# Batch 0's states alone ahead of x, identity products between TensorE's early steps, VectorE's order kept into batch 1, and stores of the state rows by quarters

## The chip, the cores and the metric

The kernel runs on one core of one Trainium2 chip. A core has five engines with a queue of instructions each: TensorE (PE in the profile; PEld is its loading of the stationary operand), VectorE (DVE), ScalarE (ACT), GpSimd (POOL) and SyncE (SP), which here only issues transfers. Engines run at the same time and wait for one another through semaphores; each works through its own queue in order. The metric is the device time of one execution in microseconds, as the median of several runs. The profile is of one execution.

## The reference

Two blocks are joined. The first reads x (8 batches, 8 heads, 512 tokens, 64 values) and 32 states per batch and head; the second is a feed-forward layer over 4608 rows.

```python
scores = scale * x @ state.T;  a = softmax(scores);   xread = a @ state     # 512 rows per batch
scores2 = scale * state @ x.T; a2 = softmax(scores2); sread = a2 @ x        # 32 rows per batch
x = concat([xread, sread], rows), heads side by side                        # (8*544, 512)
h = x @ w_in                                                                # 512 -> 2048
g = where(h > 0, h, exp(min(h, 0)) - 1)
out = g @ w_out                                                             # 2048 -> 512
```

The two weight matrices arrive as 64-bit numbers (a 128x512 piece is 512 KB); everything is computed in 32 bits.

## The kernel before, in words

A batch's 512 token rows go through attention, a first product (`ffn1`, 16 parts `F:0` to `F:15` of 128 hidden columns) and a second product with w_out. The states are folded into the first product: M = states x w_in (`make_m`), copied to `m_sb` (`copy_m`, `copy_half`), is multiplied by the turned attention weights `aT`. After each part ScalarE makes the exponential (`exp_part`, two ACTIVATEs), and VectorE the maximum (`max_part`, into `g_all`). Nearly every instruction is recorded at the helper's line L100, so rows are told apart by their tiles.

**Batch 0** (`first_batch`) runs while the weights arrive. Its order is written out by hand as a list, `plan`, and TensorE, VectorE, ScalarE and GpSimd keep that order (`InOrder`). The steps, for batch b and half g:

- `kT`, `kTc`: turn the states on TensorE, copy them to `kT` on VectorE. `x:b.i`, `xc:b.i`: turn half of x, copy on ScalarE. `sc`: scores. `mx`, `tr`, `tm`: column maximum, transpose, row maximum on VectorE; `ps`, `pm`: subtract and scale on GpSimd; `ae`, `te`: exponentials on ScalarE; `sd`, `su`: sums and reciprocals on VectorE; `tt`: transpose to `aT`. `sT`, `sTc`, `sr`, `src`: turn the state-side weights, copy, multiply by x, keep.
- `w:k.1`, `w:k.2`: conversion of weight piece k, three ScalarE and four VectorE instructions. After each `w:k.2` comes `fetch`, which issues one more piece on SP's queue. Pieces 0-3 are w_in for parts 0-3, 4-7 for parts 4-7, 8-11 the first four of w_out, and so on.
- `M`, `Mc`: M for two parts, and its copy. `F`, `R`, `E`, `O`: a part of the first product, its exponential, its maximum, and its share of the second product, which adds into banks 0 to 3 (`ffn2_row`).

At the end banks 0 to 3 are copied to `o_sb` and stored.

**Batches 1 to 7** (`batch`) do all 16 parts of the first product, then the second product by Strassen's scheme (`Strassen`, and in it `Second`), which needs sums and differences of quarters of w_out (`weight_sum` into `t_w`, and `Second.weights` into `t`, `b` and parts of w_in). Those are made in batch 1. `F` parts of batch 1 rotate through banks 4, 5, 3. In the second product, the attention of the next batch is put between its steps (`attention`, `hooks`). From batch 1 on VectorE, ScalarE and GpSimd no longer keep the written order: a scheduler may pull a ready instruction forward. TensorE and SP keep theirs throughout.

**The state rows** of all batches come last (`states`): one first product, one Strassen product of seven products in two halves of 256 rows (`half.o_sb[0]`, `[1]`), and eight stores on SP's queue, one a batch.

TensorE's pair of banks 6 and 7 is shared by the turned states, x, scores, the half M's and the state read of batch 0, so each of these steps waits for the copy of the one before.

Of the kernel before, what the change touches and what calls it, by code (L numbers as in the profile page):

```python
# [10 lines left out]
FP32 = mybir.dt.float32  # L11
# [14 lines left out]
def kernel(  # L26
# [15 lines left out]
    B, H, S, D = x.shape  # L42
    NS = state.shape[2]
    DM, DF = moe_w_in.shape
    P = 128
# [39 lines left out]
    def bank(i):  # L85
        return psum[:, i]

    def pair(i):

        return psum[:, i : i + 2]  # L90
# [19 lines left out]
    def transpose(out, in_):  # L110


        for t in range(2):
            rows = slice(t * 64, (t + 1) * 64)
            tensor.transpose(out[:, t], in_[rows], ident[rows, rows], tile_position=(t * 64, 0))
# [22 lines left out]
                out=x_t[b][:, r].rearrange("p (h d) -> p h d", d=D), in_=x_v[:, r]  # L138
            )

    def load_states():
        raw = work.tile([P, B, G, D], FP32, tag="w", name="s_sb")
        s_v = state.rearrange("b (m c) n d -> m c n b d", c=G)
        for m in range(NP):
            for c in range(G):
                (sync, scalar)[c].dma_start(out=raw[m * NS : (m + 1) * NS, :, c], in_=s_v[m, c])
        return raw

    def turn_states(raw):
        ps = st["k_ps"] = pair(6).rearrange("p t (b q) -> p t b q", q=64)  # L150
        for b in range(B):
            transpose(ps[:, :, b], raw[:, b].rearrange("p c d -> p (c d)"))

    def load_weights(src):
        _, n, k = src.shape
# [281 lines left out]
    def combine(out, x, y, op=ALU.subtract):  # L437
        for o, i, j in zip(out, x, y):
            vector.tensor_tensor(out=o, in0=i, in1=j, op=op)
# [3 lines left out]
    b11, b12, b21, b22 = (halves(w_k[:, :, e, h]) for e in range(2) for h in range(2))  # L443
    t_w = {3: b12}

    def weight_sum(i):

        if i != 3:
            t_w[i] = [
                work.tile([P, FO // 4, DM // 2], FP32, tag="w", name="t_w") for k in range(2)  # L450
            ]
        x, y = {1: (b12, b11), 2: (b22, t_w.get(1)), 3: (b22, b12), 4: (b21, t_w.get(2))}[i]
        combine(t_w[i], x, y)

    class Second:

# [232 lines left out]
    def first_batch():  # L689

        plan = """
            kT kTc x:0.0 xc:0.0 w:0.1 x:0.1 xc:0.1 w:0.2 w:1.1 sc:0 mx:0.1 w:2.1 tr:0.1 tr:0.0
            tm:0.1 w:3.1 tm:0.0 ps:0.1 mx:0.0 w:1.2 ps:0.0 ae:0.1 ae:0.0 te:0.1 sT:0 sd:0.0 sd:0.1
            te:0.0 su:0.1 sTc:0 su:0.0 pm:0.1 w:4.1 M:0.0.0 w:3.2 pm:0.0 Mc:0.0.0 w:7.1 sr:0 tt:0.1
            tt:0.0 w:4.2 F:0 src:0 w:8.1 w:2.2 F:1 R:0 w:5.1 E:0 M:0.0.1 w:8.2 Mc:0.0.1 R:1 F:2  # L700
            w:5.2 w:9.1 O:0 E:1 w:10.1 w:9.2 R:2 F:3 w:10.2 w:6.1 M:0.1.0 O:1 E:2 Mc:0.1.0 w:6.2 R:3
            w:12.1 E:3 F:4 w:7.2 w:11.1 O:2 w:12.2 w:13.1 R:4 w:11.2 M:0.1.1 F:5 w:14.1 w:13.2 O:3
            R:5 Mc:0.1.1 E:4 w:16.1 E:5 w:14.2 F:6 w:17.1 M:0.2.0 w:16.2 F:7 R:6 w:15.1 E:6 O:4
            w:17.2 Mc:0.2.0 w:18.1 w:15.2 F:8 R:7 w:18.2 O:5 w:21.1 E:7 R:8 w:21.2 M:0.2.1 w:19.1
            O:6 E:8 w:23.1 w:19.2 Mc:0.2.1 F:9 w:23.2 w:24.1 O:7 w:25.1 w:24.2 w:20.1 w:25.2 F:10
            R:9 O:8 w:20.2 w:22.1 E:9 R:10 w:22.2 M:0.3.0 w:26.1 F:11 E:10 O:9 Mc:0.3.0 w:26.2 R:11
            w:27.1 E:11 M:0.3.1 w:29.1 w:27.2 F:12 O:10 R:12 w:29.2 Mc:0.3.1 w:30.1 E:12 F:13 w:31.1
            w:30.2 O:11 R:13 w:31.2 w:28.1 E:13 x:1.0 w:28.2 F:14 xc:1.0 x:1.1 R:14 F:15 xc:1.1 E:14
            sc:1 R:15 O:12 mx:1.0 mx:1.1 ae:1.0 tr:1.0 ae:1.1 tr:1.1 tm:1.0 sT:1 tm:1.1 ps:1.0 O:13
            sd:1.0 sTc:1 sd:1.1 E:15 ps:1.1 te:1.0 su:1.0 te:1.1 pm:1.0 su:1.1 sr:1 pm:1.1 tt:1.0  # L710
            O:14 src:1 tt:1.1 M:1.0 O:15 Mc:1.0
        """.split()
        make_identity(nc, ident)
        o_ps = [bank(c) for c in range(R)]
        order = [lambda k=k: load_w_in(0, k) for k in range(4)]
        for c in range(1, FC + 1):
            if c < FC:
                order += [lambda c=c, k=k: load_w_in(c, k) for k in range(4)]
            order += [lambda fo=fo: load_w_out(fo) for fo in range(4 * c - 4, 4 * c)]
        w, h, e = [], {}, {}  # L720

        def fetch():
            if len(w) < len(order):
                w.append(order[len(w)]())
            elif 1 not in x_t:
                load_x(1, [sync])
                for c in range(FC):
                    k = slice(2 * c, 2 * c + 2)
                    sync.dma_start(out=w_in_mem[:, k], in_=w_in[:, k])

        raw_states = load_states()
        load_x(0, [sync, scalar])
        for k in range(NRAW - 1):
            fetch()
        groups = {
            "mx": column_max, "tr": turn_scores, "ae": column_exp, "tm": row_max,
            "ps": row_subtract, "te": row_exp, "su": row_sum, "pm": row_scale,
            "tt": turn_tokens, "sd": column_total,
        }
        whole = {  # L740
            "sc": scores, "sT": turn_state, "sTc": copy_state, "sr": state_read,
            "src": keep_read,
        }
        for step in plan:
            name, _, num = step.partition(":")
            num = [int(i) for i in num.split(".") if i]
            if name == "kT":
                turn_states(raw_states)
            elif name == "kTc":
                vector.tensor_copy(out=kT.rearrange("p b (t q) -> p t b q", t=2), in_=st["k_ps"])  # L750
                fetch()
            elif name in groups:
                groups[name](*num)
            elif name in whole:
                whole[name](*num)
            elif name == "w":
                (convert_1, convert_2)[num[1] - 1](*w[num[0]])
                if num[1] == 2:
                    fetch()
            elif name == "F":  # L760
                h[num[0]] = ffn1(0, num[0])
            elif name == "R":
                e[num[0]] = exp_part(h[num[0]])
            elif name == "E":
                max_part(num[0], e[num[0]], h[num[0]])
            elif name == "O":
                ffn2_row(o_ps, num[0])
            elif name == "x":
                turn_x(*num)
            elif name == "M":  # L770
                make_m(*num)
                if len(num) == 2:
                    make_m(1, 1, first=4)
            elif name == "xc":
                copy_x(*num)
            else:
                assert name == "Mc", step
                if len(num) == 3:
                    copy_half(*num)
                else:  # L780
                    for g in range(G):
                        copy_m(*num, g, scalar.copy)
        for g in range(G):
            copy_m(1, 1, g, scalar.copy)
        for i in range(2):
            o_sb = opool.tile([P, 2, DM], FP32, tag="o", name="o_sb")
            for c in range(2):
                (scalar.copy, vector.tensor_copy)[c](out=o_sb[:, c], in_=o_ps[2 * i + c])
            store(0, i, o_sb)

    def batch(b):
        for fo in range(FO):
            elu(ffn1(b, fo), fo)
            if fo == FO // 4 + 1:
                for c in (2, 3):
                    make_m(b, c, first=6 if c == 2 else 0)
            if FO // 4 + 1 <= fo < FO // 4 + 5:
                c, g = divmod(fo - FO // 4 - 1, G)
                copy_m(b, 2 + c, g, vector.tensor_copy)
            if b == 1 and fo % 4 == 3:  # L800
                weight_sum((1, 2, 4, 3)[fo // 4])
            if b > 1 and fo == FO // 4 + 2:
                fetch_w_in(0, 0)
        nxt = b + 1 < B
        hooks = attention(b + 1) if nxt else [turn_read]
        if nxt and b > 0:
# [21 lines left out]
    def states():  # L828
        for i in second.values():
            i.restore()  # L830
        for fo in range(FO):
            ffn1_state(fo)
        half = Strassen(1)
        half.sums()
        for f in half.steps():
            f()
        for b in range(B):
            c, i = divmod(b, P // NS)
            sync.dma_start(
                out=out_b[b, S:SB], in_=half.o_sb[c][i * NS : (i + 1) * NS].rearrange("p n c -> p (n c)")  # L840
            )

    first_batch()
    load_x(2, [sync])
    for e in (vector, scalar, gpsimd):
        e.on = False
    for b in range(1, B):
        batch(b)
# [31 lines left out]
```

## Time and profile before

| | us |
|---|---|
| median of 9 runs | 763.64 (762.88 to 764.50) |
| the profiled execution | 762.98 |
| its span, first to last instruction | 761.2 |
| TensorE busy | 730.3 (96%) |
| VectorE busy | 467.1 (61%) |
| ScalarE busy | 311.9 (41%) |
| GpSimd busy | 35.1 (5%) |
| mean granted TensorE clock | 0.995 of full |

How to read it: a row of the timeline has start, duration, engine, operation, output<-inputs, shape and count, and in brackets the idle time before it and what ended that. A row of the waits has the total, the number of times and the longest. A row of the stretches has start and end, length, then the busy time of PE, PEld, DVE, ACT and POOL with the number of instructions, the granted TensorE clock as a share of full, the busy share of the transfer engines and GB/s. A 32-bit product shows as two records. Ends of matmuls are modelled, so a duration may overlap the next row by a little.

### The profile page before, as it was taken

Reading aid. Unit: us, or ns where it says so; the run is one execution under the profiler, and the core shown is the slowest. Engines: PE = TensorE matmul, PEld = TensorE weight load, DVE = VectorE, ACT = ScalarE, POOL = GpSimd, SP = SyncE. Lnnn points to the kernel's source line nnn. Section 1 sums busy time; section 2 is a strip of 40 time slices with the busy share of each in tenths; the row PEclk is TensorE's granted clock in tenths of the full one; section 3 lists DMA queues with packets and bytes.
Section 4 is the critical chain, followed back from the end, with each engine's and each line's share of the span. In section 5 each row is a group of like instructions: output and inputs, shape, how many; then the busy total and the mean of one; then the engine's idle time right before and its main releaser. Section 6 shows DMA issues by size and latency. Waiting matters only on the chain.

```text
span 761.2 us, 11358 instructions
## 1 busy us (share of the span) xinstructions
PE 730.3 (96%) x4640; PEld 504.8 (66%) x4640; DVE 467.1 (61%) x855; ACT 311.9 (41%) x575; POOL 35.1 (5%) x38
## 2 busy tenths in 40 slices
PE   3599999899999999999999999999999999999996
PEld 1234444367964798468946895579746994699885
DVE  2999989748336673667555764667356745566330
ACT  4799874553036311652055303631265106410420
POOL 0200002002000200001000200020001100000000
PEclk9899999999999999999999999999999999999999
DMA  9655900402212221213030231222122003003001
GB/s 281 228 198 205 319 13 1 111 1 111 56 56 112 111 56 56 111 64 103 29 138 1 112 57 65 101 112 57 56 110 90 24 31 135 1 1 139 28 1 28
DMA packets 49172, 66.79 MB, mean 88 GB/s; under 512 B 36832, under 2 KB 36832, under 8 KB 45280
## 3 DMA queue, kind: packets, MB, share of 16 engines
q1 hardware_dynamic: 45952, 65.28, 25.3%
q10 hardware_dynamic: 3168, 0.79, 0.5%
q8 instruction: 36, 0.59, 0.3%
q14 instruction: 16, 0.13, 0.1%
HBM read 52.95 MB, written 13.11 MB: 87 GB/s over the span
## 4 chain that ended last, share of the span: by engine, by line
PE 90%; DVE 6%; ACT 1%; DMA 1%; issue 0%; ACTq 0%; DVEq 0%
PE ps L100 90%; DVE t_w L100 1%; DVE w_in L100 1%; DMA x_sb<-in_x_dram 1%; DVE total_t L100 1%; DVE s L100 0%; DVE g_all L100 0%; DVE w_out L100 0%; DMA s_sb<-in_state_dram 0%; ACT raw L100 0%; DVE top L100 0%; ACT e_sb L100 0%; DVE aT L100 0%; DVE m_sb L100 0%; DVE top_t L100 0%; DVE o_sb L100 0%
## 5 line engine op out<-in xcount | busy, mean ns | idle before, releaser
L100 PE MATMUL ps<-aT,m_sb 128*128 128x512 f32 x512 | 229.2, 601 | 6.6 <-DVE aT L100 3.4
L100 PE MATMUL ps<-w_out,g_all 128*128 128x256 f32 (+2 forms) x1088 | 234.7, 367 | 0.7
L100 PEld LDWEIGHTS ps<-w_out,g_all 128*128 128x128 f32 x1088 | 175.7, 191 | 54.3 <-issue 36.0
L100 PEld LDWEIGHTS ps<-aT,m_sb 128*128 128x128 f32 x512 | 96.3, 192 | 129.7 <-issue 116.9
L100 ACT ACTIVATE e_sb<-ps 128x512 f32<-128x512 f32 (+1 forms) x144 | 82.4, 572 | 224.3 <-PE ps L100 206.6
L100 DVE SCALAR_TENSOR_TENSOR g_all<-e_sb,ps 128x512 f32<-128x512 f32 (+1 forms) x144 | 94.3, 656 | 116.4 <-ACT e_sb L100 116.4
L100 DVE TENSOR_TENSOR o_sb<-o_sb,ps 128x128 f32<-128x128 f32 (+2 forms) x170 | 52.7, 310 | 76.2 <-PE ps L100 74.4
L100 PE MATMUL ps<-t_w,s 128*128 128x256 f32 (+1 forms) x480 | 89.3, 338 | 0.0
L100 ACT ACTIVATE e_sb<-e_sb 128x512 f32<-128x512 f32 (+1 forms) x144 | 87.3, 606 | 4.5
L100 PEld LDWEIGHTS ps<-t_w,s 128*128 128x128 f32 x480 | 77.2, 191 | 7.3 <-DVE o_sb L100 0.2
L100 ACT COPY o_sb<-ps 128x512 f32<-128x512 f32 (+2 forms) x52 | 21.3, 423 | 121.8 <-PE ps L100 114.7
L100 ACT ACTIVATE raw<-raw 128x512 f32<-128x512 uint32 x64 | 43.5, 680 | 1.0
L100 POOL TENSOR_TENSOR t_sb<-t_sb,top_t 128x512 f32<-128x512 f32 x16 | 17.7, 1109 | 532.8 <-DVE top_t L100 532.8
L100 DVE TENSOR_TENSOR s<-s,g_all 128x512 f32<-128x512 f32 (+1 forms) x36 | 32.1, 896 | 14.4 <-PE ps L100 14.2
L100 DVE TENSOR_TENSOR g_all<-g_all,s 128x512 f32<-128x512 f32 (+1 forms) x36 | 31.9, 885 | 9.6 <-PE ps L100 9.6
L100 PE MATMUL ps<-w_in,kT 64*32 64x512 f32 (+1 forms) x576 | 33.6, 554 | 0.0
L100 DVE TENSOR_TENSOR g_all<-g_all 128x512 f32<-128x512 f32 (+1 forms) x36 | 32.2, 895 | 0.5
L100 PE MATMUL ps<-t_w,g_all 128*128 128x128 f32 (+1 forms) x240 | 32.1, 282 | 0.0
L100 DVE TENSOR_TENSOR s<-g_all 128x512 f32<-128x512 f32 (+1 forms) x36 | 31.6, 894 | 0.5
L100 PE MATMUL ps<-w_in,s 128*128 128x128 f32 x240 | 30.7, 275 | 0.0
L100 PEld LDWEIGHTS ps<-t_w,g_all 128*128 128x128 f32 x240 | 29.8, 192 | 0.5
L100 DVE TENSOR_REDUCE top<-ps 128x1 f32<-128x512 f32 x16 | 10.9, 684 | 29.1 <-PE ps L100 29.1
(78 smaller groups left out, 576.4 us busy)
## 6 DMA issues: line engine op xcount, KB each, us to landing
w_in<-w_in_mem SPq DMA_DIRECT2D x26, 1024.0 KB, 6.2
raw<-in_moe_w_in_dram SPq DMA_DIRECT2D x16, 512.0 KB, 5.8
raw<-in_moe_w_out_dram SPq DMA_DIRECT2D x16, 512.0 KB, 3.3
out_dram<-o_sb SPq DMA_DIRECT2D x16, 512.0 KB, 2.6
x_sb<-in_x_dram SPq DMA_DIRECT2D x30, 256.0 KB, 4.7
w_in_mem<-w_in SPq DMA_DIRECT2D x4, 1024.0 KB, 6.4
x_sb<-in_x_dram ACTq DMA_DIRECT2D x2, 256.0 KB, 5.5
out_dram<-o_sb SPq DMA_DIRECT2D x8, 64.0 KB, 1.7
```

Source lines behind the costliest of these rows:

```text
L100: ins = getattr(self.engine, name)(*args, **kw)
```

## The change

- Batch 0's states are loaded alone (`load_states(0, 1, ...)`, one issue on SP's and one on ScalarE's queue, into a tile of their own). The other seven batches' states are loaded by eight issues on SP when twelve weight pieces have been fetched, and turned and copied by two new steps, `kU` and `kUc`.
- Seven weight pieces are fetched ahead of the plan, not six plus one after `kTc`.
- `Z:n` is new: n products of the identity by itself into bank 3, which the first `O` overwrites. There are three, of 14, 8 and 14. The plan has a new order throughout.
- Bank 3 and 2 are copied and stored ahead of bank 1 and 0.
- VectorE keeps its written order to the end of batch 1's first product (`vector.on = False` moves there), and `weight_sum` is called eight times for half the work each.
- The state rows are stored by quarters, four stores after each of four of the Strassen product's seven steps; after the last step two go over ScalarE's queue.

```diff
--- before.py
+++ after.py
@@ -138,18 +138,34 @@
                 out=x_t[b][:, r].rearrange("p (h d) -> p h d", d=D), in_=x_v[:, r]
             )
 
-    def load_states():
-        raw = work.tile([P, B, G, D], FP32, tag="w", name="s_sb")
-        s_v = state.rearrange("b (m c) n d -> m c n b d", c=G)
-        for m in range(NP):
-            for c in range(G):
-                (sync, scalar)[c].dma_start(out=raw[m * NS : (m + 1) * NS, :, c], in_=s_v[m, c])
+    state_v = state.rearrange("b (m c) n d -> c m n b d", c=G)
+
+    def load_states(b0, b1, engines=None):
+
+        shape = [P, b1 - b0, G, D]
+        if b0 == 0:
+            raw = cpool.tile(shape, FP32, name="s_first")
+        else:
+            raw = work.tile(shape, FP32, tag="w", name="s_sb")
+        for c in range(G):
+            if b0 == 0:
+                engines[c % len(engines)].dma_start(out=raw[:, 0, c], in_=state_v[c, :, :, 0])
+                continue
+            for m in range(NP):
+                sync.dma_start(
+                    out=raw[m * NS : (m + 1) * NS, :, c], in_=state_v[c, m, :, b0:b1]
+                )
         return raw
 
-    def turn_states(raw):
-        ps = st["k_ps"] = pair(6).rearrange("p t (b q) -> p t b q", q=64)
-        for b in range(B):
+    def turn_states(raw, b0, b1):
+        ps = st["k_ps"] = pair(6)[:, :, : (b1 - b0) * 64].rearrange("p t (b q) -> p t b q", q=64)
+        for b in range(b1 - b0):
             transpose(ps[:, :, b], raw[:, b].rearrange("p c d -> p (c d)"))
+
+    def copy_states(b0, b1):
+        vector.tensor_copy(
+            out=kT[:, b0:b1].rearrange("p b (t q) -> p t b q", t=2), in_=st["k_ps"]
+        )
 
     def load_weights(src):
         _, n, k = src.shape
@@ -443,14 +459,15 @@
     b11, b12, b21, b22 = (halves(w_k[:, :, e, h]) for e in range(2) for h in range(2))
     t_w = {3: b12}
 
-    def weight_sum(i):
-        if i != 3:
+    def weight_sum(i, half):
+
+        if i != 3 and half == 0:
             t_w[i] = [
                 work.tile([P, FO // 4, DM // 2], FP32, tag="w", name="t_w") for k in range(2)
             ]
         x, y = {1: (b12, b11), 2: (b22, t_w.get(1)), 3: (b22, b12), 4: (b21, t_w.get(2))}[i]
-        combine(t_w[i], x, y)
+        k = slice(half, half + 1)
+        combine(t_w[i][k], x[k], y[k])
 
     class Second:
 
@@ -693,22 +710,23 @@
 
 
 
+
         plan = """
-            kT kTc x:0.0 xc:0.0 w:0.1 x:0.1 xc:0.1 w:0.2 w:1.1 sc:0 mx:0.1 w:2.1 tr:0.1 tr:0.0
-            tm:0.1 w:3.1 tm:0.0 ps:0.1 mx:0.0 w:1.2 ps:0.0 ae:0.1 ae:0.0 te:0.1 sT:0 sd:0.0 sd:0.1
-            te:0.0 su:0.1 sTc:0 su:0.0 pm:0.1 w:4.1 M:0.0.0 w:3.2 pm:0.0 Mc:0.0.0 w:7.1 sr:0 tt:0.1
-            tt:0.0 w:4.2 F:0 src:0 w:8.1 w:2.2 F:1 R:0 w:5.1 E:0 M:0.0.1 w:8.2 Mc:0.0.1 R:1 F:2
-            w:5.2 w:9.1 O:0 E:1 w:10.1 w:9.2 R:2 F:3 w:10.2 w:6.1 M:0.1.0 O:1 E:2 Mc:0.1.0 w:6.2 R:3
-            w:12.1 E:3 F:4 w:7.2 w:11.1 O:2 w:12.2 w:13.1 R:4 w:11.2 M:0.1.1 F:5 w:14.1 w:13.2 O:3
...
-            O:14 src:1 tt:1.1 M:1.0 O:15 Mc:1.0
+            kT kTc x:0.0 xc:0.0 x:0.1 w:0.1 xc:0.1 w:0.2 w:1.1 sc:0 Z:14 tr:0.0 tr:0.1 w:2.1 tm:0.0
+            tm:0.1 ps:0.0 w:3.1 mx:0.1 mx:0.0 ps:0.1 w:1.2 ae:0.0 te:0.1 ae:0.1 sd:0.0 su:0.1 w:5.1
+            M:0.0.0 sd:0.1 pm:0.1 w:3.2 Mc:0.0.0 te:0.0 sT:0 w:4.1 tt:0.1 su:0.0 sTc:0 w:5.2 pm:0.0
+            w:8.1 Z:8 sr:0 tt:0.0 src:0 w:2.2 Z:14 F:0 w:6.1 F:1 w:8.2 R:0 M:0.0.1 R:1 E:0 Mc:0.0.1
+            E:1 O:0 w:9.1 w:4.2 w:10.1 w:9.2 F:2 w:7.1 w:6.2 M:0.1.0 F:3 R:2 w:7.2 Mc:0.1.0 O:1
...
+            F:14 sTc:1 sd:1.1 ps:1.1 te:1.0 sr:1 R:14 su:1.0 F:15 te:1.1 pm:1.0 E:14 src:1 su:1.1
+            O:14 R:15 tt:1.0 pm:1.1 E:15 tt:1.1 M:1.0 O:15 Mc:1.0
         """.split()
         make_identity(nc, ident)
         o_ps = [bank(c) for c in range(R)]
@@ -720,6 +738,8 @@
         w, h, e = [], {}, {}
 
         def fetch():
+            if len(w) == 12 and len(raw_states) == 1:
+                raw_states.append(load_states(1, B))
             if len(w) < len(order):
                 w.append(order[len(w)]())
             elif 1 not in x_t:
@@ -728,9 +748,9 @@
                     k = slice(2 * c, 2 * c + 2)
                     sync.dma_start(out=w_in_mem[:, k], in_=w_in[:, k])
 
-        raw_states = load_states()
+        raw_states = [load_states(0, 1, [sync, scalar])]
         load_x(0, [sync, scalar])
-        for k in range(NRAW - 1):
+        for k in range(NRAW):
             fetch()
         groups = {
             "mx": column_max, "tr": turn_scores, "ae": column_exp, "tm": row_max,
@@ -744,11 +764,13 @@
         for step in plan:
             name, _, num = step.partition(":")
             num = [int(i) for i in num.split(".") if i]
-            if name == "kT":
-                turn_states(raw_states)
-            elif name == "kTc":
-                vector.tensor_copy(out=kT.rearrange("p b (t q) -> p t b q", t=2), in_=st["k_ps"])
-                fetch()
+            if name in ("kT", "kU"):
+                turn_states(raw_states[name == "kU"], *((0, 1) if name == "kT" else (1, B)))
+            elif name in ("kTc", "kUc"):
+                copy_states(*((0, 1) if name == "kTc" else (1, B)))
+            elif name == "Z":
+                for i in range(num[0]):
+                    matmul(bank(3)[:, :P], ident, ident, start=True, stop=True)
             elif name in groups:
                 groups[name](*num)
             elif name in whole:
@@ -782,9 +804,10 @@
                         copy_m(*num, g, scalar.copy)
         for g in range(G):
             copy_m(1, 1, g, scalar.copy)
-        for i in range(2):
+
+        for i in (1, 0):
             o_sb = opool.tile([P, 2, DM], FP32, tag="o", name="o_sb")
-            for c in range(2):
+            for c in (1, 0):
                 (scalar.copy, vector.tensor_copy)[c](out=o_sb[:, c], in_=o_ps[2 * i + c])
             store(0, i, o_sb)
 
@@ -797,10 +820,11 @@
             if FO // 4 + 1 <= fo < FO // 4 + 5:
                 c, g = divmod(fo - FO // 4 - 1, G)
                 copy_m(b, 2 + c, g, vector.tensor_copy)
-            if b == 1 and fo % 4 == 3:
-                weight_sum((1, 2, 4, 3)[fo // 4])
+            if b == 1 and fo % 2 == 1:
+                weight_sum((1, 2, 4, 3)[fo // 4], fo % 4 // 2)
             if b > 1 and fo == FO // 4 + 2:
                 fetch_w_in(0, 0)
+        vector.on = False
         nxt = b + 1 < B
         hooks = attention(b + 1) if nxt else [turn_read]
         if nxt and b > 0:
@@ -832,17 +856,25 @@
             ffn1_state(fo)
         half = Strassen(1)
         half.sums()
-        for f in half.steps():
+        for n, f in enumerate(half.steps()):
             f()
-        for b in range(B):
-            c, i = divmod(b, P // NS)
-            sync.dma_start(
-                out=out_b[b, S:SB], in_=half.o_sb[c][i * NS : (i + 1) * NS].rearrange("p n c -> p (n c)")
-            )
+            quarter = {1: (0, 0), 4: (1, 1), 5: (1, 0), 6: (0, 1)}.get(n)
+            if quarter is None:
+                continue
+            c, q = quarter
+            cols = slice(q * DM // 2, (q + 1) * DM // 2)
+            for i in range(P // NS):
+                engine = scalar if n == 6 and i % 2 else sync
+                engine.dma_start(
+                    out=out_b[c * P // NS + i, S:SB, cols],
+                    in_=half.o_sb[c][i * NS : (i + 1) * NS, 0, cols],
+                )
 
     first_batch()
     load_x(2, [sync])
-    for e in (vector, scalar, gpsimd):
+    for e in (scalar, gpsimd):
         e.on = False
     for b in range(1, B):
         batch(b)
```

More of the change, by code (lines that the diff above doesn't have):

```diff
@@ L702, in first_batch @@
-            w:12.1 E:3 F:4 w:7.2 w:11.1 O:2 w:12.2 w:13.1 R:4 w:11.2 M:0.1.1 F:5 w:14.1 w:13.2 O:3
[L703 to L707, printed above, removed]
@@ L708, in first_batch @@
-            w:30.2 O:11 R:13 w:31.2 w:28.1 E:13 x:1.0 w:28.2 F:14 xc:1.0 x:1.1 R:14 F:15 xc:1.1 E:14
-            sc:1 R:15 O:12 mx:1.0 mx:1.1 ae:1.0 tr:1.0 ae:1.1 tr:1.1 tm:1.0 sT:1 tm:1.1 ps:1.0 O:13
-            sd:1.0 sTc:1 sd:1.1 E:15 ps:1.1 te:1.0 su:1.0 te:1.1 pm:1.0 su:1.1 sr:1 pm:1.1 tt:1.0
-            O:14 src:1 tt:1.1 M:1.0 O:15 Mc:1.0
+            kT kTc x:0.0 xc:0.0 x:0.1 w:0.1 xc:0.1 w:0.2 w:1.1 sc:0 Z:14 tr:0.0 tr:0.1 w:2.1 tm:0.0
+            tm:0.1 ps:0.0 w:3.1 mx:0.1 mx:0.0 ps:0.1 w:1.2 ae:0.0 te:0.1 ae:0.1 sd:0.0 su:0.1 w:5.1
@@ new lines, in first_batch @@
+            M:0.0.0 sd:0.1 pm:0.1 w:3.2 Mc:0.0.0 te:0.0 sT:0 w:4.1 tt:0.1 su:0.0 sTc:0 w:5.2 pm:0.0
+            w:8.1 Z:8 sr:0 tt:0.0 src:0 w:2.2 Z:14 F:0 w:6.1 F:1 w:8.2 R:0 M:0.0.1 R:1 E:0 Mc:0.0.1
+            E:1 O:0 w:9.1 w:4.2 w:10.1 w:9.2 F:2 w:7.1 w:6.2 M:0.1.0 F:3 R:2 w:7.2 Mc:0.1.0 O:1
+            w:11.1 E:2 R:3 w:10.2 M:0.1.1 w:12.1 F:4 w:11.2 Mc:0.1.1 O:2 R:4 E:3 w:14.1 w:12.2 F:5
+            w:13.1 E:4 w:14.2 O:3 R:5 w:16.1 E:5 w:13.2 F:6 w:17.1 w:16.2 M:0.2.0 R:6 F:7 w:18.1
+            w:17.2 O:4 Mc:0.2.0 w:18.2 w:20.1 kU w:15.1 E:6 O:5 w:20.2 w:21.1 w:15.2 w:19.1 F:8 kUc
@@ new lines, in first_batch @@
+            O:6 R:8 w:21.2 R:7 w:22.1 E:7 M:0.2.1 E:8 F:9 w:19.2 Mc:0.2.1 w:23.1 M:0.3.0 F:10 w:22.2
+            w:24.1 O:7 w:23.2 R:9 Mc:0.3.0 E:9 w:25.1 w:24.2 M:0.3.1 F:11 Mc:0.3.1 R:10 w:25.2 O:8
+            R:11 E:10 w:26.1 E:11 F:12 w:29.1 w:26.2 O:9 w:30.1 w:29.2 w:27.1 F:13 w:30.2 w:28.1
+            O:10 w:27.2 R:13 R:12 w:28.2 x:1.0 w:31.1 O:11 E:12 E:13 xc:1.0 w:31.2 x:1.1 O:12 xc:1.1
+            sc:1 O:13 mx:1.1 mx:1.0 ae:1.1 tr:1.0 ae:1.0 tr:1.1 sd:1.0 sT:1 tm:1.0 tm:1.1 ps:1.0
```

## The prediction

> **What bounds the kernel now.** I read the page first: TensorE is busy for 96% of the span, and the chain that ended last is TensorE's for nine tenths.
>
> ```profile
> PE 730.3 (96%) x4640; PEld 504.8 (66%) x4640; DVE 467.1 (61%) x855; ACT 311.9 (41%) x575; POOL 35.1 (5%) x38
> PE 90%; DVE 6%; ACT 1%; DMA 1%; issue 0%; ACTq 0%; DVEq 0%
> ```
>
> So only places where TensorE stands still, or runs slowly, are worth anything. TensorE's waits before 45 us add up to some 21 us; there are three between 125 and 165 us, and the timeline shows where:
>
> ```profile
> PE ps L100 <- DVE o_sb L100: 1.8, 1, 1.8
> PE ps L100 <- DVE g_all L100: 0.6, 2, 0.3
> ```
>
> ```profile
> 31.64 6.01 PE L100 MATMUL ps<-aT,m_sb 128*128 128x512 f32 x8 [3.35 <-DVE aT L100]
> 37.58 0.66 PE L100 MATMUL ps<-w_in,kT 64*32 64x256 f32 x16
> 39.10 1.99 PE L100 MATMUL ps<-aT,m_sb 128*128 128x512 f32 x4 [0.86 <-ACT m_sb L100]
> ...
> 135.39 7.13 PE L100 MATMUL ps<-aT,m_sb 128*128 128x512 f32 x16 [1.81 <-DVE o_sb L100]
> ```
>
> The fourth row is batch 1 waiting for the copy that empties bank 3. The first is `F:0` and `F:1`: eight records in 6.01 us, where four cost 1.99 us later. The stretches give the clock:
>
> ```profile
> 30.00:36.00 6.00, 4.36 (x5) 1.85 (x6) 5.79 (x11) 1.76 (x3) 0.00 (x0) 0.50 0.68 229
> 38.00:40.00 2.00, 1.14 (x14) 0.49 (x3) 1.93 (x4) 1.97 (x5) 0.00 (x0) 1.00 0.41 155
> ```
>
> Half clock in the first, full in the second. From 39 to 133 us TensorE never waits. The end, SyncE's timeline:
>
> ```profile
> 755.27 3.65 SPq L100 DMA_DIRECT2D out_dram<-o_sb  x8
> ```
>
> Eight stores issued one after another, after the last product; the span ends at 761.2.
>
> **The Trainium skill.** "TensorE: Matmul & The Clock Gate", Part 1, says that an idle TensorE drops to half clock and returns to full after about 3.4 us of sustained work; the trace agrees (clock 0.50 over 30 to 36 us, full by 38). Its Part 4 adds that transposes do not count as such work in the same way; no row here separates that. "SBUF — State Buffer", "SBUF: two separate sides", says that VectorE instructions with two SBUF inputs or a two-port mode exclude GpSimd, whole instructions at a time; here a 128x1024 weight sum takes 1.21 us alone and 1.70 to 1.94 us while GpSimd works (116.2 to 119.2). "DMA: Bandwidth & Descriptors", "Issuing engines are not separate DMA queues", says that a second issuing engine saves only the issuing time; the trace has 3.65/8 = 0.46 us for that, all of it exposed at the end.
>
> **1. States first, x sooner.** Removed ahead of x: four state issues a queue (0.74 to 2.59 on SP), and SP's wait to 3.23. Now one issue a queue stands there, so x is issued at about 1.2: 2.0 us earlier. Before, x landed last at 10.46; I take 8.4. Bounds: 7.0, since some 0.46 MB of states also leaves the way, at 171 to 241 GB/s; 9.1, since weight loads now follow x directly and share the way. `kTc` shrinks from 1.22 to about 0.25 us, but ended at 8.06, before x: worth nothing on the path.
>
> The path from x to `F:0`, with rows of before. x to the scores' end: 10.46 to 17.2, spacing 6.75 us, so 15.2. VectorE then: two transposes 1.2, two row maxima 1.2, two column maxima with their scaling 1.7 (19.3); weight conversion `w:1.2` 2.25, made of 0.43+0.43+0.69+0.69 (21.6); `sd`, `su` 1.4 (23.0); `sd`, `w:3.2` with GpSimd beside it 3.3 (26.3, GpSimd adds about 0.7, as in its 2.96 at 21.30); `tt:0.1` 0.6; `su:0.0` 1.05 (28.0); `w:5.2` 2.95 (30.9); `tt:0.0` 0.6: 31.5. `F:0` began at 31.64. So the 2.0 us are spent: one conversion more stands ahead of `F:0`, and `F:0` doesn't move.
>
> **2. Identity products.** Thirty-six products of 128x128. Sixteen records of that shape take 1.95 us at full clock, two records a product: 0.22 us each, 0.45 at half. `Z:14` after the scores runs 15.3 to 19.8, under VectorE's maxima; `Z:8` (1.8) lies under ScalarE's copy of the turned states; the last `Z:14` (3.1) follows the state read, 28.4 to 31.5, and ends just when `tt:0.0` does. It is hidden with nothing to spare: if it runs cold, about half of it at 0.45, `F:0` is 1.7 us late. I take it warm. Then `F:0`, `F:1` cost 3.5 us, not 5.94 (31.64 to 37.58): -2.4. The 0.86 us wait for `m_sb` at 39.10 goes too, since `O:0` now stands there; but `O:0` itself waits 1.1 us, because VectorE does `w:2.2`, `w:8.2`, `E:0` from 31.5 (2.25+2.25+0.68 = 36.7, TensorE free at 35.6): +0.3.
>
> **3. The other seven batches' states** move into the busy stretch. TensorE: 14 transposes at 1.22/32 = 0.5 us, unhidden. VectorE: a copy of 896 elements a row, 1.05 us of an engine 95% busy there. SP: eight more issues, 3.7 us, ahead of raw load 12. They wait for a buffer that the third conversion frees (26.3), so load 12 is issued near 30 and lands near 35; ScalarE asks for it only past 50. The cover is 15 us. GpSimd's queue gets nothing. Through plan order and this copy I expect TensorE waits of 0.6 us between 40 and 125. Sum: +1.1.
>
> First batch: -2.4+0.3+1.1 = -1.0; from both bounds of x -1.9 to -0.4, with a cold clock up to +1.0.
>
> **4. Bank 3 first, VectorE in order.** Before, weight sums made for later were pulled into 116 to 131, so bank 3's copy came at 132.86. Now VectorE, whose queue is empty by about 121, copies bank 3 as `O:15` ends, in 0.68 us; `F:0` and `F:1` of batch 1 cover it with 3.5 us: -1.8. The sums go into batch 1's first product: eight halves at 1.2 us (GpSimd is idle there), 9.7 us; with 16 `max` parts at 0.6, four copies at 0.6 and those sums that the scheduler still pulls in, some 27 us of VectorE in 29.5. Queued behind one of them is a wait. After the third half stand three 128x512 sums into w_in (0.6 each), then `E:6`, then the second copy of M's third quarter. From batch 1's start as zero: `E:5` ends 12.2, copy 12.8, half 14.0, three sums 15.8, `E:6` 16.4, copy 17.0. `F:8` needs it and could begin at eight products, 13.8, plus M's 1.9: 15.7. New wait 1.3. The same reckoning on the order of before gives 2.3 us of waits where 2.4 were measured. The old two (0.24, 0.35) go: -0.6. VectorE is then clear about 40 us in, as the next batch's scores come: hidden, no spare. Sum: -1.8-0.6+1.3 = -1.1; bounds -1.9 to -0.5.
>
> **5. Stores by quarters.** Sixteen stores of 32 KB instead of eight of 64. Twelve go out under the last two products (3.45 us each, four issues 1.85). After the last copy, two issues on SP and two on ScalarE's queue: 0.95 us, not 3.65: -2.7. What follows, 761.2-758.92 = 2.3 us, I keep: stores of 64 KB landed in 1.7 us and those of 512 KB in 2.6, so halving the size does little. Bounds -3.1 to -2.2.
>
> Sum: -1.0-1.1-2.7 = -4.8, on 762.98 of the profiled execution (span 761.2 and 1.8 around it): 758.2. The runs' median lies 0.66 above it: 758.8.
>
> **Rivals.**
> A, the clock stays low in the head (chance 0.2): gaps of 1.5 to 2 us lie between the identity groups, and transposes may not hold the clock. For it: `sT` took 1.97 us at 22.25, against 1.04 later. Against: the last `Z:14` follows a state read without a gap. Head +1.0, not -1.0: 760.8.
> B, the early transfers are quicker and the new wait at `F:8` doesn't show (0.2): x at 7.0 gives -1.9, step 4 -2.4: 756.6. Against: 17.0 and 15.7 are worked from rows that hardly vary.
> C, slower (0.07): VectorE's in-order queue in batch 1. Halves at 1.8 us and sums at 0.9, as beside GpSimd, would stop TensorE at `F:8`, `F:11`, `F:13` and `F:15` for 3.8 us by the same reckoning, and leave VectorE 8.5 us late for the next scores. Steps 1 to 3 and 5 give -3.7, and -2.4 of old waits goes: it decides only if batch 1 waits over 7.6 us, about twice that; at 8 us, 765.5. GpSimd's rows are at 116 to 129, and the next ones after 172: against it.
> D, the first batch is set by VectorE's conversions, 95% busy, and what the stores save is all (0.08): steps 1 to 4 nothing, 760.9.
> Forecast as worked: 0.45.
>
> A measurement of this kernel can tell about 0.2%, 1.5 us, from no change. Faster takes the forecast, A, B and D but their upper edges: 0.90; same 0.05, slower 0.05 (part of C comes out even). The range: from B with the stores' better bound (756.2) to A with x at 9.1 and the stores' worse one (761.9, cut to 761.8).
>
> **What would show it.** x's last transposes at 8.4; `F:0` near 31.5 in 3.5 us for eight records, clock 1.00 there; `O:15` ending near 129.0, not 129.99; no wait for `o_sb` in batch 1, one of about 1.3 us for `m_sb` at its ninth product; SP's last two issues within 1 us, and 2.3 us to the end. Wrong: half clock at `F:0`, an `m_sb` or `g_all` wait over 3 us, or stores of 32 KB that land later than those of 64.

## The result, and the profile after

| | before | changed |
|---|---|---|
| median, us | 763.62 (762.50 to 764.50, 29 runs) | 757.73 (756.57 to 759.60, 9 runs) |
| profiled execution, us | 762.98 | 759.74 |
| span, us | 761.2 | 757.9 |

The ratio is 0.9925, 95% interval 0.9917 to 0.9933: 5.9 us faster, where 763.64 to 758.8 was forecast. The changed kernel spreads over 3 us, and its profiled execution is at the long end of that, 2.0 us above the median. So a second profile of the same program is used beside it, "changed, second profile", whose execution took 757.24 us (span 755.4). The difference between the two turns out to be the main lesson.

The page of the first profile, its busy times and chain:

```profile
PE 737.7 (97%) x4712; PEld 514.4 (68%) x4712; DVE 465.0 (61%) x856; ACT 312.3 (41%) x575; POOL 34.4 (5%) x38
PE 88%; DVE 8%; ACT 1%; DMA 1%; issue 0%; SPq 0%; DVEq 0%; ACTq 0%
```

TensorE is busy 7.4 us longer in a shorter span: 72 records of identity products are in it. Its head is told by the stretches of the same profile (after the five busy times stand the granted clock, the share of the transfer engines and GB/s):

```profile
22.00:24.00 2.00, 1.29 (x16) 0.30 (x14) 1.93 (x5) 1.97 (x5) 0.00 (x0) 1.00 0.28 113
24.00:26.00 2.00, 0.69 (x3) 0.69 (x4) 1.85 (x7) 2.00 (x5) 1.30 (x1) 0.65 0.71 256
26.00:28.00 2.00, 2.00 (x12) 2.00 (x11) 1.93 (x4) 1.97 (x5) 0.00 (x0) 0.50 0.04 14
28.00:30.00 2.00, 2.00 (x11) 2.00 (x11) 1.90 (x6) 1.97 (x5) 0.47 (x1) 0.50 0.32 74
30.00:32.00 2.00, 2.00 (x68) 1.69 (x66) 1.93 (x3) 0.73 (x2) 0.58 (x1) 0.65 0.54 121
```

The granted clock is 1.00 up to about 24.6 (0.65 over two microseconds is 0.6 us at full and 1.4 at half) and half until about 31.4. (Below, warm is full clock and cold is half.) The timeline of TensorE in the same execution:

```profile
9.79 1.01 PE L100 MATMUL ps<-ident,x_sb 64*128 64x64 f32 x12 [1.44 <-DMA x_sb<-in_x_dram]
...
16.65 3.90 PE L100 MATMUL ps<-ident 128*128 128x128 f32 x28
21.85 0.62 PE L100 MATMUL ps<-w_in,kT 64*32 64x256 f32 x2 [1.29 <-ACT a_s L100]
...
25.31 1.97 PE L100 MATMUL ps<-ident,a_s 128*128 128x128 f32 x8 [1.45 <-ACT m_sb L100]
27.07 3.62 PE L100 MATMUL ps<-ident 128*128 128x128 f32 x16
30.62 1.45 PE L100 MATMUL ps<-x_sb,aT_s 128*32 128x64 f32 x64
32.01 3.39 PE L100 MATMUL ps<-ident 128*128 128x128 f32 x28
35.23 3.60 PE L100 MATMUL ps<-aT,m_sb 128*128 128x512 f32 x8
```

And in the second profile:

```profile
9.24 0.80 PE L100 MATMUL ps<-ident,x_sb 64*128 64x64 f32 x10 [0.18 <-DMA x_sb<-in_x_dram]
...
15.88 4.99 PE L100 MATMUL ps<-ident 128*128 128x128 f32 x28
21.09 0.62 PE L100 MATMUL ps<-w_in,kT 64*32 64x256 f32 x2 [0.21 <-ACT a_s L100]
...
24.56 1.09 PE L100 MATMUL ps<-ident,a_s 128*128 128x128 f32 x8 [1.46 <-ACT m_sb L100]
25.49 1.95 PE L100 MATMUL ps<-ident 128*128 128x128 f32 x16
27.42 1.14 PE L100 MATMUL ps<-x_sb,aT_s 128*32 128x64 f32 x64
28.49 3.39 PE L100 MATMUL ps<-ident 128*128 128x128 f32 x28
32.23 3.70 PE L100 MATMUL ps<-aT,m_sb 128*128 128x512 f32 x8 [0.34 <-DVE aT L100]
37.31 3.70 PE L100 MATMUL ps<-w_out,g_all 128*128 128x512 f32 x8 [0.79 <-DVE g_all L100]
```

The row with `ident,a_s` is `sT`, the one with 16 records `Z:8`: 1.97 and 3.62 us in the first profile, 1.09 and 1.95 in the second. The last group (28 records before `F:0`) takes 3.39 us in both, so it is warm in both. The chain makes `F:0` start at 35.23 or at 32.23. In the first profile VectorE's last `aT` is this row of its timeline:

```profile
32.23 0.70 DVE L100 STREAM_TRANSPOSE aT<-t_sb 128x512 f32<-128x512 f32 x1
```

It ends at 32.93, so the identity products alone hold `F:0` for 2.3 us there. In the second the same row starts at 31.47, `F:0` waits 0.34 us for it and the products hold nothing. In both, eight records cost 3.6 to 3.7 us, not 6.01.

The waits of TensorE from 45 us to the end, in both profiles, are one row:

```profile
PE ps L100 <- DVE m_sb L100: 0.8, 1, 0.8
```

Bank 3's wait is gone. The stages of the three profiles, from the timelines:

| ends at, us | before | changed, first profile | changed, second profile |
|---|---|---|---|
| last `O` of batch 0 (batch 1's `F:0` begins) | 129.99 | 131.47 | 128.97 |
| batch 1's first product | 162.73 | 162.05 | 159.54 |
| last copy of the state rows | 755.24 | 754.55 | 752.04 |
| span | 761.2 | 757.9 | 755.4 |

Differences to before in the second profile: first batch -1.02, batch 1's first product -2.17 (32.74 to 30.57), all batches after it 0.0, stores -2.6 (5.96 to 3.36): -5.8, close to the 5.9 of the medians. In the first profile the first batch is +1.48, the rest the same. The end of the first profile, SyncE's and ScalarE's timelines:

```profile
751.17 4.18 SPq L100 DMA_DIRECT2D out_dram<-o_sb  x6
754.18 0.37 ACT L100 COPY o_sb<-ps 128x256 f32<-128x256 f32 x1 [9.99 <-PE ps L100]
754.58 0.85 ACTq L100 DMA_DIRECT2D out_dram<-o_sb  x2
```

SP's six end at 755.35, ScalarE's two at 755.43: 0.9 us behind the copy, not 3.65.

### The profile page after: what moved, and what is told of

The parts are those of the page before. It is cut to its first block, busy times and chain, and to the rows that moved or that the text cites. A ratio compares the mean times of both kernels' runs of the same rounds, so it can differ in the third digit from the quotient of the medians.

```text
span 757.9 us, 11509 instructions
## 1 busy us (share of the span) xinstructions
PE 737.7 (97%) x4712; PEld 514.4 (68%) x4712; DVE 465.0 (61%) x856; ACT 312.3 (41%) x575; POOL 34.4 (5%) x38
## 4 chain that ended last, share of the span: by engine, by line
PE 88%; DVE 8%; ACT 1%; DMA 1%; issue 0%; SPq 0%; DVEq 0%; ACTq 0%
PE ps L100 88%; DVE w_in L100 3%; DVE w_out L100 2%; DMA x_sb<-in_x_dram 1%; DVE g_all L100 1%; DVE s L100 0%; ACT raw L100 0%; ACT e_sb L100 0%; ACT xT L100 0%; DVE top L100 0%; ACT a_s L100 0%; SPq L100 0%; DVE t_sb L100 0%; DVE m_sb L100 0%; DVE top_t L100 0%
## 5 line engine op out<-in xcount | busy, mean ns | idle before, releaser
L100 PE MATMUL ps<-aT,m_sb 128*128 128x512 f32 x512 | 226.2, 595 | 0.8 <-DVE m_sb L100 0.8
L100 DVE TENSOR_TENSOR g_all<-g_all 128x512 f32<-128x512 f32 (+1 forms) x36 | 32.2, 894 | 0.5
L100 PEld LDWEIGHTS ps<-w_in,s 128*128 128x128 f32 x240 | 28.7, 192 | 0.0
```

The lines of the kernel that those rows point to most:

```text
L100: ins = getattr(self.engine, name)(*args, **kw)
```

## The experiments

Each kernel was timed beside the kernel before on the same chip, and its ratio is to that; three chips were used, so ratios, times 763.4, are compared rather than medians. Their intervals are about 1 us to either side. The changed kernel's ratio is taken as 0.9921, from its second set of runs; with the 0.9925 of the first set each loss below is 0.3 us smaller and each gain 0.3 us larger. Each run has one profile, of one execution.

**The changed kernel again**, unedited.

> The changed kernel once more, so that it stands beside the others on one chip. If the parts undone one at a time (1.1 for the head, 1.4 for step 4, 1.9 for the stores) hold all there is, it lies at 763.7 - 4.4 = 759.3; if they overlap or the first nine runs were typical, at 757.7. It should spread over some 3 us, from 756.5 to 759.7, since its head depends on when the clock drops.

757.38 (757.14 to 758.50), ratio 0.9921 (0.9908 to 0.9933): 6.0 us. The second profile above is of this run. So the nine first runs were typical.

**Without identity products.**

```diff
-  sc:0 Z:14 tr:0.0 ... w:8.1 Z:8 sr:0 ... w:2.2 Z:14 F:0
+  sc:0 tr:0.0 ...      w:8.1 sr:0 ...     w:2.2 F:0
```

> The changed kernel (757.7) without its 36 identity products; nothing else is touched. Theory 1, the identity products earn their place by keeping the clock up: F:0 and F:1 then run at half clock (5.9 us instead of 3.6), and the first batch ends some 1 to 2 us later: 758.7 to 759.7. Rival, they stand on the path: in the profile of the changed kernel the second VectorE transpose of the tokens ends at 32.9 and F:0 begins at 35.2, behind identity products at half clock; without them F:0 begins near 32.9 or before, the 2.3 us pay for the cold F:0 and F:1, and the time is the same within 1 us: 757 to 758.5.

759.05 (758.08 to 759.58), ratio 0.9934 (0.9921 to 0.9948). TensorE's timeline and the stretch around its second row:

```profile
27.84 1.93 PE L100 MATMUL ps<-x_sb,aT_s 128*32 128x64 f32 x64 [0.87 <-ACT aT_s L100]
32.67 5.95 PE L100 MATMUL ps<-aT,m_sb 128*128 128x512 f32 x8 [2.90 <-DVE aT L100]
```

```profile
34.00:38.00 4.00, 4.00 (x6) 1.49 (x6) 3.17 (x7) 1.23 (x2) 0.00 (x0) 1.00 0.94 346
```

`F:0` and `F:1` take 5.95 us again, about as long as at half clock in the kernel before (6.01), though the clock column reads 1.00. Batch 0's last `O` ends at 131.28 here: 2.3 us later than in the second profile of the changed kernel, 0.45 of it because x was later (the scores began at 14.44, not 13.99), and about as late as in its first (131.47). So in these three profiles the products save some 1.9 us where the clock stays up and next to nothing where it drops. On the ratios 0.0013 of 763.4, 1.0 us, is left, no more than the error, and at the edge of both theories: the runs alone don't decide between them.

**Old stores.**

```diff
-  engine.dma_start(out=out_b[..., cols], ...)   # four after each of four steps
+  sync.dma_start(out=out_b[b, S:SB], ...)       # eight after the last step
```

> The changed kernel with the eight stores of the state rows at the end on one queue, as before. Theory: issuing is what was exposed; the last copy to the end of the span was 5.96 us before and 3.35 us after, so 757.7 + 2.6 = 760.3. Rival, the smaller stores merely ended in a luckier place and the gain lies elsewhere: under 1 us, 758.5 or less.

759.62 (759.31 to 760.28), ratio 0.9949 (0.9936 to 0.9961): 0.0028, 2.1 us behind the changed kernel. In its timeline the last copy ends at 751.98 and the span at 757.8: 5.8 us against 3.36. The theory holds; the rival's bound of 1 us is passed.

**VectorE and the bank order as before.**

```diff
-  vector.on = False      # after batch 1's first product; half sums at odd parts; banks 3, 2, 1, 0
+  vector.on = False      # after batch 0; whole sums at every fourth part; banks 0, 1, 2, 3
```

> The changed kernel with VectorE's written order given up before batch 1, sums of w_out in whole pieces every fourth part, and bank 0 first: step 4 undone alone. Theory: the stretch from the last product of batch 0 to the end of batch 1's first product grows again from 30.6 to 32.7 us: 757.7 + 2.1 = 759.8, with the wait for o_sb of about 1.8 us back. Rival, the wait comes from how the first batch ends in the new order and not from step 4: no wait for o_sb, 757.7 within 0.7.

759.10 (758.93 to 760.81), ratio 0.9946 (0.9933 to 0.9958): 0.0025, 1.9 us. The size is the theory's, the place is not. TensorE's timeline:

```profile
121.52 3.70 PE L100 MATMUL ps<-w_out,g_all 128*128 128x512 f32 x8 [1.32 <-DVE g_all L100]
...
148.50 1.98 PE L100 MATMUL ps<-aT,m_sb 128*128 128x512 f32 x4 [0.24 <-DVE g_all L100]
150.84 10.57 PE L100 MATMUL ps<-aT,m_sb 128*128 128x512 f32 x24 [0.35 <-DVE g_all L100]
```

No wait for `o_sb`; instead `O:14` waits 1.32 us for `E:14`, because three sums of w_out were pulled ahead of that maximum on VectorE:

```profile
118.14 1.41 DVE L100 TENSOR_TENSOR t_w<-w_out 128x1024 f32<-128x1024 f32 x1
...
119.55 1.21 DVE L100 TENSOR_TENSOR t_w<-w_out,t_w 128x1024 f32<-128x1024 f32 x1
...
120.85 0.62 DVE L100 SCALAR_TENSOR_TENSOR g_all<-e_sb,ps 128x512 f32<-128x512 f32 x1
```

In both plans, this one and that of before, the pulled-up sums delay something worth 1 to 2 us, but not the same thing.

This run's profile is also a second one in which the clock dropped in the head. Its timeline and stretches:

```profile
15.33 4.52 PE L100 MATMUL ps<-ident 128*128 128x128 f32 x28
20.53 0.62 PE L100 MATMUL ps<-w_in,kT 64*32 64x256 f32 x2 [0.68 <-ACT a_s L100]
...
25.29 3.23 PE L100 MATMUL ps<-ident 128*128 128x128 f32 x16
```

```profile
26.00:30.00 4.00, 4.00 (x82) 3.79 (x82) 3.86 (x8) 3.81 (x9) 1.05 (x1) 0.75 0.33 74
```

`Z:8` takes 3.23 us, and half clock lasts until about 28.0.

**The old head** with the new VectorE order and stores (the kernel before, plus steps 4 and 5).

```diff
-  raw_states = [load_states(0, 1, [sync, scalar])]; plan with kU, Z
+  raw_states = load_states(); plan of before
```

> The kernel before with step 4 and the quarter stores, but the old head: states together, old plan, no identity products. Theory 1, the head as changed is worth what my sum says: 758.7, 1.0 over the changed kernel. Theory 2, as the one profile has it (last product of batch 0 ends at 131.5, not 130.0), the new head costs 1.5 us: 756.2. If the head's worth depends on the clock's phase, the runs here spread less than the 3 us of the changed kernel's.

758.81 (758.65 to 759.37), ratio 0.9938 (0.9925 to 0.9950): 0.0017, 1.3 us behind the changed kernel. It spreads over 0.7 us, the changed kernel over 1.4 to 3.0. The three parts undone give 1.3 + 1.9 + 2.1 = 5.3 of 6.0 (against the first set of runs 1.0 + 1.6 + 1.8 = 4.4 of 5.7). With an error of 1 us on each, that they add up without overlap is likely and not shown.

**Bank order alone**, on the kernel before.

```diff
-  for i in range(2): ... for c in range(2):
+  for i in (1, 0):   ... for c in (1, 0):
```

> The kernel before with one edit: banks 3 and 2 are copied and stored ahead of 1 and 0. VectorE's order is free after batch 0, as before. Theory, most of step 4 is the bank order alone: bank 3's copy takes the place at 132.86 us where bank 1's stood, the wait of 1.81 us for o_sb falls to about 0.5, and 763.7 falls to 762.2. Rival, the written order is what counts: the weight sums still run ahead of the copy, which is late in any order, and the time stays within 0.5 of 763.7.

763.59 against 763.34, ratio 1.0001 (0.9993 to 1.0009): nothing. VectorE's timeline says why:

```profile
134.46 0.68 DVE L100 TENSOR_TENSOR t<-t_w,t 128x512 f32<-128x512 f32 x1
135.06 1.28 DVE L100 COPY o_sb<-ps 128x512 f32<-128x512 f32 x2
```

The sums run first, then both banks' copies one behind the other; the wait for `o_sb` is 1.81 us as before. Without the written order the bank order buys nothing.

**All of x on SP's queue.**

```diff
-  load_x(0, [sync, scalar])
+  load_x(0, [sync])
```

> The changed kernel with all four loads of x on the queue of the weight loads, so that no weight load can stand beside x on another queue. Theory, x landed at 9.8 and not at 8.4 because weight loads on one queue share the way with x on the other: x's last transposes begin before 9.0 and the time falls by up to 0.8. Rival, x is late because its data starts late and small pieces move at 200 to 250 GB/s whatever stands beside them: the last x at 9.3 to 10, no gain, or up to 1 us of loss from two issues more in a row.

756.62 (756.24 to 757.01), ratio 0.9909 (0.9895 to 0.9922). The last of x is turned from 8.67, and each load lands 3.6 to 4.9 us after its issue, where the changed kernel's took 4.6 to 6.8 in the second profile and 5.8 to 7.6 in the first. That fits x and the weight loads competing across the two queues, but one trace doesn't prove it: the landing varies by itself (in the run with VectorE as before, x on two queues was turned last from 8.38), and the edit also moves the first weight load from 2.85 to 4.73. All four runs lie below all five of the changed kernel on that chip, though the two intervals overlap.

**More identity products.**

```diff
-  sc:0 Z:14 tr:0.0 ... te:0.0 sT:0
+  sc:0 Z:20 tr:0.0 ... te:0.0 Z:6 sT:0
```

> The changed kernel with 20 identity products in the first group instead of 14, and a fourth group of 6 between the first M and the turning of the state-side weights. Theory, the clock drops near 24.7 us because TensorE stands still for some 3.4 of the 4.8 us from 20.5 to 25.3; with the gaps filled it stays up, the second and last group run at 0.22 us a product, F:0 begins by 32.5 in each run: 756.8, with a spread under 2 us. Rival, the drop comes anyway and the added products, at half clock, stand in the way: 758.5 to 760.

757.56 (757.24 to 758.58), ratio 0.9924 (0.9911 to 0.9938). In its profile TensorE is busy from 16.1 to 32.2 without a gap, and `F:0` begins at 32.48, behind `aT`. The second profile of the changed kernel, without the added products, has the same warm head, and the spread is hardly smaller (1.3 us against 1.4). Nothing is gained and nothing lost: the time is 0.8 us above the theory's, and below the rival's range. Whether the added products prevent the drop of the clock stays open: this one profile is warm, but so are seven of the nine whose first group has 14 products.

**States ahead of x.**

```diff
-  raw_states = [load_states(0, 1, [sync, scalar])]
+  raw_states = [load_states(0, 1, [sync, scalar]), load_states(1, B)]
```

> The changed kernel with the other seven batches' states issued on SP directly behind batch 0's and ahead of x, not after twelve weight pieces; the turning and the copy of them stay late. Theory, states in the way of x are what delayed it: eight issues of 0.46 us stand ahead of SP's two loads of x, x lands last at 10.5 or later, some 1.0 to 2.0 us behind the changed kernel, and the time rises by as much: 758.4 to 759.4. Rival, what counts is the shorter copy to kT and the plan, and where the states' transfer stands does not matter: 757.4 within 0.5.

759.81 (759.12 to 760.62), ratio 0.9951 (0.9938 to 0.9963): 0.0030, 2.3 us. x on SP is issued at 6.00 (1.51 in the changed kernel), its last part turned from 10.89, and `F:0` starts at 33.99 with a warm clock. So eight issues ahead of x are worth about 2 us of the head, as the theory had it.

**The second set of sums held in order too.**

```diff
-  lambda: second[5].weights(t_w[1])
+  lambda: (on(), second[5].weights(t_w[1]), off())   # vector.on set around each of the four
```

> The changed kernel with VectorE's written order held for the second set of weight sums too, so that none of them can be pulled ahead of batch 1's maxima. Theory, the wait of 0.76 us for m_sb at the ninth product comes from the three sums into w_in that stand before the seventh maximum: without them there no wait is left in batch 1's first product, 757.4 - 0.8 = 756.6. Rival, the copy would be late anyway behind the third half: a wait of 0.3 or more stays, or the sums make TensorE wait where they now stand, between 180 and 205 us: 757.4 or more.

757.31 (756.84 to 757.82), ratio 0.9920 (0.9906 to 0.9934), the changed kernel's within the error. Batch 1's first product has no wait row left, but a new one appears at 210 us, a little behind where the rival put it. TensorE's timeline:

```profile
140.96 17.80 PE L100 MATMUL ps<-aT,m_sb 128*128 128x512 f32 x40
...
210.11 1.16 PE L100 MATMUL ps<-b,s 128*128 128x128 f32 x8 [0.60 <-DVE o_sb L100]
```

Theory right on the cause of the `m_sb` wait, the rival right on the time.

**The last four stores on one queue.**

```diff
-  engine = scalar if n == 6 and i % 2 else sync
+  engine = sync
```

> The changed kernel with the last four stores all on SP's queue. Theory, only the issues after the last copy are exposed: four in a row instead of two beside two, 2 x 0.45 = 0.9 us more: 758.3. Rival, the landing decides and the issues are hidden under it: 757.4 within 0.3.

757.79 (757.49 to 758.16), ratio 0.9925 (0.9912 to 0.9937): 0.3 us, within the error; the trace decides. From the last copy's end to the span's end it is 3.7 us (752.28 to 756.0) against 3.36: two issues cost 0.4, not 0.9. The last issue ends at 754.01, and what follows is 2.0 us; with two queues it was 2.5 (755.43 to 757.9). So part of the issue time is hidden; it may lie under the landing of the stores before, which isn't shown.

**Both edits together.**

> Two of the edits together on the changed kernel: all four loads of x on SP's queue, and the written order held for the second set of weight sums. If both are worth what they should be alone, 757.4 - 0.8 - 0.8 = 755.8; if the sums hurt where they then stand, 756.6 or more.

756.54 (756.41 to 756.72), ratio 0.9909 (0.9895 to 0.9922): the time of x on SP alone, and the wait of 0.60 us for `o_sb` is in this trace too. These two kernels are the fastest measured: some 6.8 us below the kernel before, and some 0.9 below the changed one by the ratios, whose intervals still overlap; two of the changed kernel's first nine runs (756.57) were as low.

## Why the prediction was right, and where it was not

**Sum.** Forecast 758.8, measured 757.73, in the range; the direction and the parts hold. The profiled execution was forecast at 758.2 and took 759.74: the clock was taken as warm, and in that execution it was not. The second profile (757.24) is below the forecast by what step 4 gave more. Some of the agreement is luck, as steps 2 to 4 show: misses of about half a microsecond cancel there.

**Step 1, x sooner: mis-sized.** x is issued at 1.51, where about 1.2 was said: on SP the first state issue takes 0.72 us and on ScalarE's queue 1.15, not 0.46. I took 8.4 for its landing, with 9.1 as the late bound. It was 9.79 in the profile and 8.4 to 9.7 in the seven other profiles with the same head loads. The term that fell short is the landing. The weight loads' share of the way, which I put into the bound and not into the value, is the likely reason (8.67 and 8.53 in the two profiles with all of x ahead of them on one queue), but is not shown. That `F:0` would not move, because the plan spends what x gains, came out: 32.23 against 31.64, 0.6 us late.

**Step 2, identity products: right when warm, and whether they are warm differs between executions.** A product takes 0.24 us at full clock (1.95/8, 3.39/14), not the 0.22 that I divided out, so the last group takes 3.4 us, not 3.1. "Nothing to spare" was correct: `aT` is 0.34 us behind the products in the second profile, and the products 2.3 us behind `aT` in the first. I priced a cold last group at 1.7 us. What ran cold in the first profile were the steps ahead of it: `sT` (1.97 us against 1.09 in the second), `Z:8` (3.62 against 1.95) and part of `sr` (1.45 against 1.14). `F:0` starts 3.0 us later there, 0.7 of it by the later `aT` and 2.3 by the products. `F:0` and `F:1` at 3.6 to 3.7 us: right, in both. `O:0` waits 0.79, forecast 1.1.

First batch: -1.02 in the warm profile, -1.0 forecast. This match is partly luck: `F:0` came 0.6 us late (32.23 against 31.64), which was forecast at nothing, and the 0.6 us of waits forecast for step 3 did not come. In the cold profile it is +1.48, beyond rival A's +1.0. A's low clock came in two of the nine profiles with these groups, and not quite as A had it, since `F:0` itself was warm there.

**Step 3, the other states: right in kind, too dear.** `kU` takes 0.65 us (0.5 said), raw load 12 is issued at 32.2 and 31.0 in the two profiles (30 said). TensorE waits for nothing between 45 and 125, so the 0.6 us of waits was too much.

**Step 4: right in kind, too small.** I forecast -1.1 with a best bound of -1.9 and it was -2.17. Bank 3's copy is as forecast: VectorE was idle and makes both copies as `O:15` ends (first profile).

```profile
131.68 1.29 DVE L100 COPY o_sb<-ps 128x512 f32<-128x512 f32 x2 [6.34 <-PE ps L100]
```

Two terms were off. The wait at `F:8` is 0.76, not 1.3. I let the whole part wait for the second copy, but its first product uses the first copy's half, and only the second waits. The rows show this: ten records, two of them `F:8`'s, then the wait.

```profile
143.75 4.56 PE L100 MATMUL ps<-aT,m_sb 128*128 128x512 f32 x10
149.07 13.14 PE L100 MATMUL ps<-aT,m_sb 128*128 128x512 f32 x30 [0.76 <-DVE m_sb L100]
```

The copy itself was later than I said, 17.5 us after batch 1's start and not 17.0 (146.50 - 128.97 in the second profile), so had the whole part waited, the wait would have been 1.8 us: one error hid part of the other.

The other term is what the old waits cost. With no wait row this stretch takes 29.91 us (128.69 to 158.60, sums held in order); with one of 0.76 it takes 30.57, with three of 2.40 together 32.74. So the three old stops cost 2.83 us, 0.4 more than their rows, and the new one 0.66, 0.1 less than its row; the reason isn't shown. The wait sits where I put it, and its cause is shown by removing it.

**Step 5, stores: right.** 2.6 in the profiles, 2.1 in the old stores' ratio, 2.7 forecast. Within it, sending twelve stores out early carries 2.2 us (5.96 to 3.72, one queue) and the second queue 0.4 (to 3.36), where equal prices of issue would have it 1.8 and 0.9.

**Rivals.** B's time (756.6) is as near as the forecast's (each 1.1 us off), but not for its reasons: x was later than its 7.0 and the wait at `F:8` did show. C did not come: the halves took 1.22 us each. D is refuted by the old stores: 4 us are left without them.

## What to carry to other kernels

Order work that is made for later behind what the present stage waits for. Here a scheduler that pulls ready sums forward moved the delay from place to place, and reordering a copy alone gained nothing. Price idle products that are to keep the clock up at half clock too (0.45 us each here, 0.24 at full): in one execution they ran slowly and held the work behind them for 2.3 us. Whether shorter groups would do better was not tried. Loads that start the chain are worth trying on the queue of the bulk loads, ahead of them: here that measured some 0.9 us faster than beside them on another queue, with intervals that still overlap.

## What the runs showed of the hardware that was not expected

The same program ran with TensorE warm in one execution and at half clock from 24.6 to 31.4 us in another, 2.5 us apart at the end of batch 0, some 0.7 of it by x. The clock's low stretches have one measure. Worked from the clock column in stretches of 0.2 us, half clock lasted 6.83 us (24.59 to 31.42) in the first profile of the changed kernel, 6.82 (29.50 to 36.32) in the kernel before, and 3.41 (24.56 to 27.98), half as long, in the run with VectorE as before. (The stretches in which it changes read 0.97 from 24.4 and 0.96 from 31.4; 0.74 from 29.4 and 0.70 from 36.2; 0.91 from 24.4 and 0.56 from 27.8.)

What the two profiles with the drop have in common is the first group of 14 identity products: it took 3.90 and 4.52 us, and 4.66 to 5.43 in the seven others, and TensorE then stood idle for 1.29 and 0.68 us, and for 0.54 at most in the others. An estimate from these lengths, with 0.226 us a record at half clock (3.62/16) and 0.121 at full (3.39/28): the clock rose near 17.8 us in those two, 6.8 us before it fell, and at 18.2 to 20.4 in the others. So a group that warms early ends early and leaves a longer gap behind it. That this gap, and not only when the clock rises, decides over the drop is not shown: no run changed one without the other.

The granted clock in the profile did not show every cold stretch. Without identity products eight records of the first product took 5.95 us, 1.6 times as long as warm, while the stretches of 30 to 38 us read 1.00 (a row is above). The old head with the new VectorE order and stores took 6.60 us for them, also at 1.00, and in the kernel before `sT` took 1.97 us at 22.25, 1.09 warm, at 1.00, before the first change in the column. In these traces durations of known shapes tell a cold TensorE; the column did so only after its first change. The mean clock of an execution doesn't tell it either: the changed kernel's two runs of 759.60 us read 0.997 and 1.000.
